# A gated scan followed by a gated convolution unit: four PSUM banks handed out in turn, x loaded apart from its gates, and part of the gated inputs moved to VectorE

## The chip, the core and the metric

The kernel runs on one core of one Trainium2 chip. The profile shows five engines that run side by side, each with its own list of instructions: TensorE (PE) for matmuls and transposes, VectorE (DVE) and ScalarE (ACT) for element-wise work, GpSimd (POOL), and SyncE (SP), which here only issues the transfers. Matmul results land in the memory PSUM, which this kernel lays out as eight banks of 2 KiB per partition; all other tiles are in the memory SBUF. The metric is the device time in microseconds. Some runs fall in a slower state; the ratios below use fast runs alone, against fast runs of the kernel before on the same chip.

## The reference

x, r_gate and i_gate have 4 x 6336 rows of 256 columns (fp32). Cut to what matters:

```
a_t     = exp(8 * sigmoid(r_gate) * log(sigmoid(a_param)))
x_gated = sqrt(max(1 - a_t*a_t, 1e-6)) * sigmoid(i_gate) * x
h_t     = a_t * h_{t-1} + x_gated_t          # scan along the rows, y = all h
gate    = sigmoid(5-tap causal convolution of y, per column)
out     = (gate * (y @ w_val)) @ w_out
```

## The kernel before

Rows come in 51 tiles of 512 rows (three have 256), most of them two to a chunk (28 chunks). The rows lie on the partitions when they are loaded, but the scan wants columns on the partitions, so TensorE transposes three times: the tanh of r (`srT`), the square root (`nT`, back to rows, to multiply it with the gated input) and the product (`xT`, for the scan). Each tile passes these stages; the names are those of the profile:

| Stage | Engine | What it does |
|---|---|---|
| load r, i, x | DMA, queue SP | three transfers of 512 KB a tile |
| tanh | ACT | both gates in one instruction (sigmoid by way of tanh) |
| u2 | POOL | (tanh(i) + 1) * x, two instructions |
| srT, exp | PE, ACT | transpose, then a |
| e | POOL | a * a |
| sq | ACT | square roots, in batches of chunks, as they need another table of functions (each load of a table took 1.28 us) |
| nT, xg | PE, DVE | transpose the root, multiply with u2 |
| xT, scan | PE, DVE | transpose the product, scan into y |
| conv, tg, val, gv | PE, ACT, PE, DVE | convolution, tanh, y @ w_val, product |
| out, osb | PE, DVE or ACT | last matmul, copy from PSUM |
| store | DMA, queue SP | 512 KB a tile |

A planner in the kernel file (a list scheduler with a cost for each job and a priority for each kind) fixes the order of each engine's instructions before anything is built. On the chip an engine waits, but does not overtake. The parts that the change touches (shortened; the comments are not in the kernel):

```python
UNITS = [3, 1, 3, 3, 2, 3, 2, 3, 2, 2, 1, 1, 1, 1]      # chunks in each batch of square roots
NS, NY, NIN, NTRI, NXG, NOSB = 10, 6, 3, 4, 3, 3        # buffers
# ... cut
        ri = inp.tile([P, 2, SUB, D], FP32, name="ri", tag="ri", bufs=NIN)
        xt = inp.tile([P, SUB, D], FP32, name="xt", tag="xt", bufs=NIN)
        nc.sync.dma_start(ri[:, 0, 0:nj, :], ...)        # r, then i, then x: always together
# ... cut
            nc.gpsimd.tensor_scalar(out=t1, in0=tri[:, 1], scalar1=1.0, scalar2=1.0, op0=ALU.mult, op1=ALU.add)
            nc.gpsimd.tensor_tensor(out=uring[:, g % NS], in0=t1, in1=xt, op=ALU.mult)
# ... cut: one PSUM bank for each purpose
            srT = psum.tile([P, CHUNK], BF16, name="srT", tag="srT", bufs=1)
            nT = psum.tile([P, SUB, D], BF16, name="nT", tag="nT", bufs=1)
            xT = psum.tile([P, CHUNK], BF16, name="xT", tag="xT", bufs=1)
            ops = psum.tile([P, 2, D], FP32, name="ops", tag="ops", bufs=1)
```

The other four banks hold the convolution (two) and y @ w_val (two), before and after.

Of the kernel before, what the change touches and what calls it, by code (L numbers as in the profile page):

```python
# [8 lines left out]
P = 128  # L9
WIN = 512  # L10
# [7 lines left out]
UNITS = [3, 1, 3, 3, 2, 3, 2, 3, 2, 2, 1, 1, 1, 1]  # L18
NS = 10
NY = 6  # L20
NIN = 3
NTRI = 4
NXG = 3
NOSB = 3

OSB = ("DDAADDDADDDDDDDDDDADADDDDDDDDADDADDDDDDDADDDDDDDADDDADDADAADADADADDDADDDDDADADADDAAAAAADDA"
       "DDDDAAAAA")

COST = dict(load=(0.1, 3.8), tanh=(0.2, 1.7), u2=(0.25, 3.15), srT=(0.05, 0.45), exp=(0.35, 0.86), e=(0.1, 1.8),
# [3 lines left out]
PRIO = dict(load=5.07, store=4.64, tanh=5.95, exp=3.94, sq=0.63, tg=0.73, srT=3.16, nT=4.77, xT=-1.91,  # L33
            conv=3.92, val=4.01, out=-0.12, e=4.3, u2=4.55, xg=-0.64, scan=3.88, gv=4.0, osb=-0.43)
# [7 lines left out]
class Shape:  # L42
# [3 lines left out]
    def __init__(self, total, seq):  # L46
        self.chunks, self.tiles, self.chunk_of = [], [], []
        self.seq, self.total = seq, total
        t = 0
        for c, parts in enumerate(CHUNKS):  # L50
            self.chunks.append((t, sum(parts), len(self.tiles), len(self.tiles) + len(parts)))
            for n in parts:
                self.tiles.append((t, n))
                self.chunk_of.append(c)
                t += n
        assert t == total
        self.apos, self.aold = self.place(NS * WIN)
        self.ypos, self.yold = self.place(NY * WIN)
        self.pieces = [(g, i) for g, (_, n) in enumerate(self.tiles) for i in range(n // (2 * P))]
# [17 lines left out]
def make_jobs(sh):  # L77


    jobs = {op: [] for op in PRIO}  # L80
# [4 lines left out]
    def job(op, eng, f, deps, cost=None):  # L85
        fix, per = COST[cost or op]
        jobs[op].append((eng, fix + per * f, [d for d in deps if d[1] >= 0]))

    for g, (_, n) in enumerate(sh.tiles):
        f = n / WIN  # L90
        c = sh.chunk_of[g]
        job("load", "DMA", f, [("tanh", g - NIN), ("u2", g - NIN)])
        job("tanh", "ACT", f, [("load", g), ("u2", g - NTRI)]
            + ([("srT", 2 * sh.chunk_of[g - NTRI] + 1)] if g >= NTRI else []))
        job("u2", "POOL", f, [("tanh", g)] + [("xg", g - NS)])
        job("nT", "PE", f, [("sq", unit_of[c]), ("xg", g - 1)])
        job("xg", "DVE", f, [("nT", g), ("u2", g)] + ([("xT", 2 * sh.chunk_of[g - NXG] + 1)] if g >= NXG else []))
        job("conv", "PE", f, [("scan", 2 * c + 1), ("tg", g - 1)])
        job("tg", "ACT", f, [("conv", g), ("gv", g - 2)])
        job("val", "PE", f, [("scan", 2 * c + 1), ("gv", g - 1), ("conv", g)])  # L100
        job("gv", "DVE", f, [("tg", g), ("val", g)] + ([("out", qlast[g - 2])] if g >= 2 else []))
        job("store", "DMA", f, [("osb", qlast[g])])
    for c, (_, n, g0, g1) in enumerate(sh.chunks):
        f = n / CHUNK
        yo = sh.yold[c]
        ylast = sh.chunks[yo][3] if yo >= 0 else -1
        for h in range(2):
            k = 2 * c + h
            job("srT", "PE", f, [("tanh", g1 - 1), ("exp", k - 1)])
            aold = ("scan", 2 * sh.aold[c] + h if sh.aold[c] >= 0 else -1)  # L110
            job("exp", "ACT", f, [("srT", k), aold])
            job("e", "POOL", f, [("exp", k), aold])
            job("xT", "PE", f, [("xg", g1 - 1), ("scan", k - 1)])
            job("scan", "DVE", f, [("xT", k), ("val", ylast - 1), ("conv", ylast)])
    for q, (g, i) in enumerate(sh.pieces):
        job("out", "PE", 1, [("gv", g), ("osb", q - 1)])
        job("osb", "DVE" if OSB[q] == "D" else "ACT", 1, [("out", q), ("store", g - NOSB)], "osb" + OSB[q])
    for u, n in enumerate(UNITS):
        size = sum(sh.chunks[c][1] for c in range(ends[u] - n, ends[u])) / CHUNK
        fix, per = COST["sq"]  # L120
        jobs["sq"].append(("ACT", fix * n + per * size, [("e", 2 * ends[u] - 1)]))
# [3 lines left out]
def make_plan(sh):  # L125


    jobs = make_jobs(sh)
    nxt = dict.fromkeys(jobs, 0)
    done, free, order, mode = {}, {}, [], "E"  # L130
    while True:
        best = None
        for op, todo in jobs.items():
# [3 lines left out]
            eng, dur, deps = todo[i]  # L137
            t = free.get(eng, 0.0)
            for d in deps:
# [5 lines left out]
            else:  # L145
                if best is None or (t, PRIO[op]) < best[:2]:
                    best = (t, PRIO[op], op, i, eng, dur)
        if best is None:
            break
        t, _, op, i, eng, dur = best  # L150
# [5 lines left out]
        done[op, i] = t + dur + (DMA_LAT if eng == "DMA" else 0.0)  # L156
        order.append((t, op, i, eng, dur))
# [3 lines left out]
    return order  # L161
# [3 lines left out]
def kernel(  # L165
# [23 lines left out]
    plan = make_plan(shape)  # L189
# [5 lines left out]
    def load(g):  # L195
# [3 lines left out]
        xt = inp.tile([P, SUB, D], FP32, name="xt", tag="xt", bufs=NIN)  # L199

        nc.sync.dma_start(ri[:, 0, 0:nj, :], rf[t0:t0 + nt, :].rearrange("(p j) d -> p j d", j=nj))
        for dst, src in ((ri[:, 1, 0:nj, :], if_), (xt[:, 0:nj, :], xf)):
            nc.sync.dma_start(dst, src[t0:t0 + nt, :].rearrange("(j p) d -> p j d", p=P))
        live["ri", g], live["xt", g] = ri, xt

    with tc.manual_schedule():
# [4 lines left out]
        for g in range(NIN):  # L211
            load(g)
# [42 lines left out]
        wo2 = const.tile([P, H, D], BF16, name="wo2")  # L255
        nc.vector.tensor_scalar(out=wo2[:], in0=wo[:], scalar1=0.5, scalar2=None, op0=ALU.mult)
# [3 lines left out]
        psum = ctx.enter_context(tc.tile_pool(name="psum", bufs=1, space=bass.MemoryType.PSUM))  # L260

        aring = rings.tile([P, H, NS * WIN], FP32, name="aring")
        ering = rings.tile([P, H, NS * WIN], FP32, name="ering")
        nring = ering[:].bitcast(BF16)
        uring = rings.tile([P, NS, SUB, D], BF16, name="uring")
# [10 lines left out]
        def op_load(g, eng):  # L276
            if g >= NIN:
                load(g)

        def op_tanh(g, eng):  # L280
            nj = tiles[g][1] // P
            ri = live.pop(("ri", g))
            tri = inp.tile([P, 2, SUB, D], BF16, name="tri", tag="tri", bufs=NTRI)
            nc.scalar.activation(out=tri[:, :, 0:nj, :], in_=ri[:, :, 0:nj, :], func=ACT.Tanh, scale=0.5)  # L284
            live["tri", g] = tri

        def op_u2(g, eng):
            nj = tiles[g][1] // P
            xt, tri = live.pop(("xt", g)), live["tri", g]
            t1 = work.tile([P, SUB, D], FP32, name="t1", tag="t1", bufs=1)  # L290
            nc.gpsimd.tensor_scalar(out=t1[:, 0:nj, :], in0=tri[:, 1, 0:nj, :], scalar1=1.0, scalar2=1.0,  # L291
                                    op0=ALU.mult, op1=ALU.add)
            nc.gpsimd.tensor_tensor(out=uring[:, g % NS, 0:nj, :], in0=t1[:, 0:nj, :], in1=xt[:, 0:nj, :],  # L293
                                    op=ALU.mult)

        def op_srT(k, eng):
            c, h = k // 2, k % 2
            srT = psum.tile([P, CHUNK], BF16, name="srT", tag="srT", bufs=1)
            transposes(srT, [(live["tri", g][:, 0], tiles[g][1] // P) for g in range(*chunks[c][2:])], h)
# [10 lines left out]
        def op_e(k, eng):  # L310
            c, h = k // 2, k % 2
            nt, a0 = chunks[c][1], shape.apos[c]
            a = aring[:, h, a0:a0 + nt]
            nc.gpsimd.tensor_tensor(out=ering[:, h, a0:a0 + nt], in0=a, in1=a, op=ALU.mult)  # L314

        def op_sq(u, eng):
            for c in range(sum(UNITS[:u]), sum(UNITS[:u + 1])):
                nt, a0 = chunks[c][1], shape.apos[c]
                nc.scalar.activation(out=nring[:, :, 2 * a0:2 * a0 + nt], in_=ering[:, :, a0:a0 + nt],  # L319
                                     func=ACT.Sqrt, scale=-0.25, bias=b025[:, 0:1])  # L320

        def op_nT(g, eng):
            c = chunk_of[g]
            n0 = 2 * shape.apos[c] + tiles[g][0] - chunks[c][0]
            nT = psum.tile([P, SUB, D], BF16, name="nT", tag="nT", bufs=1)
            for j in range(tiles[g][1] // P):
                for h in range(H):
# [4 lines left out]
        def op_xg(g, eng):  # L332
            nj = tiles[g][1] // P
            xg = work.tile([P, SUB, D], BF16, name="xg", tag="xg", bufs=NXG)
            nc.vector.tensor_tensor(out=xg[:, 0:nj, :], in0=live.pop(("nT", g))[:, 0:nj, :],  # L335
                                    in1=uring[:, g % NS, 0:nj, :], op=ALU.mult)
            live["xg", g] = xg

        def op_xT(k, eng):
            c, h = k // 2, k % 2  # L340
            xT = psum.tile([P, CHUNK], BF16, name="xT", tag="xT", bufs=1)
            transposes(xT, [(live["xg", g], tiles[g][1] // P) for g in range(*chunks[c][2:])], h)
# [73 lines left out]
        def op_out(q, eng):  # L416
            g, i = pieces[q]
            gv = live["gv", g]
            ops = psum.tile([P, 2, D], FP32, name="ops", tag="ops", bufs=1)
            for e in range(2):  # L420
                for hk in range(H):
                    nc.tensor.matmul(out=ops[:, e, :], lhsT=gv[:, 2 * i + e, hk, :], rhs=wo2[:, hk, :],  # L422
# [3 lines left out]
        def op_osb(q, eng):  # L426
            g, i = pieces[q]
            if i == 0:
                live["osb", g] = work.tile([P, SUB, D], FP32, name="osb", tag="osb", bufs=NOSB)
            dst = live["osb", g][:, 2 * i:2 * i + 2, :]  # L430
# [12 lines left out]
        ops_by_name = dict(load=op_load, tanh=op_tanh, u2=op_u2, srT=op_srT, exp=op_exp, e=op_e, sq=op_sq,  # L443
# [34 lines left out]
```

## Time and profile before

| | Before |
|---|---|
| Device time, median | 340.5 us (339.4 to 342.5, 4 runs) |
| Span of the profiled run | 338.6 us |
| Busy: ACT, POOL, PE, DVE | 302.8, 266.5, 252.6, 247.2 us |
| Moved | 104.56 MB, 309 GB/s over the span |
| Last load issued (x of the last tile) | 285.5 us |

Busy time counts all instructions of an engine, waits left out. The prediction below shows and reads the lines of the slices, of three stretches of time, and of the waits. Here is only one stretch more: from 40 to 260 us. The columns are the same as there (stretch, its length, busy time of PE, PE weight load, DVE, ACT, POOL, granted clock, DMA share, GB/s):

```profile
40.00:260.00 220.00, 177.30 (x2100) 118.63 (x2098) 173.69 (x162) 205.59 (x159) 198.54 (x114) 0.91 0.98 340
```

ACT and POOL are at 93% and 90%, DVE at 79%, and 340 GB/s move.

### The profile page before, as it was taken

What the parts mean: (1) busy time and instruction counts of PE and PEld (TensorE: products, weight loads), DVE (VectorE), ACT (ScalarE), POOL (GpSimd) and SP (SyncE); (2) the same over time, 40 slices, a digit from 0 to 9 for tenths busy, and PEclk for the clock granted to TensorE, in tenths of its full rate; (3) what the DMA queues carried; (4) which work ended last, traced back from release to release, by engine and by line L of the source; (5) the groups of instructions that cost most, each with busy time, mean ns of one, the idle gap of its engine ahead of it and who ended that gap; (6) DMA issues with size and microseconds to landing.
All of it is one profiled execution on the core that took longest, in us unless ns stands there. A gap on an engine that the chain in (4) does not pass through costs nothing.

```text
span 338.6 us, 7417 instructions
## 1 busy us (share of the span) xinstructions
PE 252.6 (75%) x2987; PEld 166.9 (49%) x2987; DVE 247.2 (73%) x251; ACT 302.8 (89%) x251; POOL 266.5 (79%) x170
## 2 busy tenths in 40 slices
PE   1122578962599699969973996995998997989894
PEld 0111444531466456646642664663665664565553
DVE  3000487840559959999973799995999998999992
ACT  6558998988979989999989899999999999999883
POOL 6699799999799867989996997998797799551100
PEclk9999997995559969999997799999999999999998
DMA  7999969999998979999999999999999999332334
GB/s 174 340 366 367 360 228 349 346 369 398 333 295 271 298 262 315 332 381 381 391 381 400 353 298 313 375 351 373 343 340 389 382 324 361 127 133 117 126 126 187
DMA packets 68432, 104.56 MB, mean 309 GB/s; under 512 B 4391, under 2 KB 55342, under 8 KB 68398
## 3 DMA queue, kind: packets, MB, share of 16 engines
q1 hardware_dynamic: 67022, 103.83, 87.6%
q0 software_dynamic: 1376, 0.26, 0.9%
q8 instruction: 23, 0.38, 0.5%
q14 instruction: 11, 0.09, 0.1%
HBM read 78.39 MB, written 25.95 MB: 308 GB/s over the span
## 4 chain that ended last, share of the span: by engine, by line
PE 28%; ACT 23%; DVE 18%; DMA 17%; issue 12%; SPq 2%; ACTq 0%; DVEq 0%
DMA ri<-in_i_gate_dram 14%; PE gp L384 10%; DVE yring L358 8%; ACT tri L284 6%; PE ops L422 5%; PE val L400 4%; ACT tg L392 4%; DVE gv L410 4%; ACT ering L319 4%; DVE osb L433 4%; PE xT L272 4%; ACT aring L306 3%; PE srT L272 3%; PE nT L328 2%; ACT L392 2%
## 5 line engine op out<-in xcount | busy, mean ns | idle before, releaser
L314 POOL TENSOR_TENSOR ering<-aring 128x1024 f32<-128x1024 f32 (+2 forms) x56 | 94.4, 1695 | 40.8 <-ACT aring L306 36.0
L293 POOL TENSOR_TENSOR uring<-t,xt 128x1024 bf16<-128x1024 f32 (+1 forms) x51 | 117.1, 2296 | 4.3
L358 DVE TENSOR_TENSOR_SCAN yring<-aring,yring,xT 128x1024 bf16<-128x1024 f32 (+5 forms) x54 | 111.1, 2057 | 11.5 <-PE xT L272 10.8
L284 ACT ACTIVATE tri<-ri 128x2048 bf16<-128x2048 f32 (+1 forms) x51 | 94.7, 1865 | 9.8 <-DMA ri<-in_i_gate_dram 9.3
L384 PE MATMUL gp<-yring,diag 64*64 64x512 bf16 (+16 forms) x1196 | 71.4, 363 | 9.3 <-ACT tg L392 7.9
L306 ACT ACTIVATE aring<-srT,khf 128x1024 f32<-128x1024 bf16 (+2 forms) x56 | 62.5, 1116 | 8.6 <-PE srT L272 5.6
L422 PE MATMUL ops<-wo,gv 128*128 128x256 bf16 x396 | 60.8, 277 | 10.2 <-DVE osb L433 6.2
L410 DVE SCALAR_TENSOR_TENSOR gv<-tg,val 128x1024 bf16<-128x1024 bf16 (+1 forms) x54 | 60.5, 1126 | 9.5 <-ACT tg L392 5.8
L335 DVE TENSOR_TENSOR xg<-nT,uring 128x1024 bf16<-128x1024 bf16 (+1 forms) x51 | 33.8, 662 | 40.9 <-PE nT L328 26.4
L272 PE MATMUL srT<-ident_b,tri 128*128 128x128 bf16 x396 | 35.9, 236 | 35.4 <-ACT tri L284 20.5
L291 POOL TENSOR_SCALAR t<-tri 128x1024 f32<-128x1024 bf16 (+1 forms) x51 | 52.0, 1020 | 10.4 <-ACT tri L284 4.5
L392 ACT ACTIVATE tg<-gp 128x1024 bf16<-128x1024 f32 (+1 forms) x51 | 51.3, 1006 | 5.0 <-PE gp L384 4.8
L433 DVE COPY osb<-ops 128x512 f32<-128x512 f32 x67 | 45.6, 680 | 13.9 <-PE ops L422 13.8
L400 PE MATMUL val<-yring,wv 128*128 128x512 bf16 (+1 forms) x204 | 51.8, 377 | 3.6 <-DVE gv L410 3.5
L319 ACT ACTIVATE ering<-ering,b 128x2048 bf16<-128x2048 f32 (+2 forms) x28 | 50.5, 1804 | 1.0
L384 PEld LDWEIGHTS <-diag 64*64 64x64 bf16 x1196 | 33.4, 111 | 34.2 <-issue 20.1
L272 PEld LDWEIGHTS <-tri 128*128 128x128 bf16 x396 | 27.9, 105 | 44.5 <-ACT tri L284 23.7
L422 PEld LDWEIGHTS <-gv 128*128 128x128 bf16 x396 | 36.1, 99 | 26.1 <-issue 15.6
L328 PE MATMUL nT<-ident_b,ering 128*128 128x128 bf16 x396 | 34.3, 235 | 12.8 <-ACT ering L319 7.6
L272 PE MATMUL xT<-ident_b,xg 128*128 128x128 bf16 x396 | 34.7, 231 | 8.7 <-DVE yring L358 6.3
L272 PEld LDWEIGHTS <-xg 128*128 128x128 bf16 x396 | 27.0, 103 | 22.0 <-issue 14.8
L328 PEld LDWEIGHTS <-ering 128*128 128x128 bf16 x396 | 27.8, 106 | 19.3 <-ACT ering L319 8.9
(31 smaller groups left out, 95.0 us busy)
## 6 DMA issues: line engine op xcount, KB each, us to landing
ri<-in_r_gate_dram SPq DMA_DIRECT2D x48, 512.0 KB, 6.7
ri<-in_i_gate_dram SPq DMA_DIRECT2D x48, 512.0 KB, 7.8
xt<-in_x_dram SPq DMA_DIRECT2D x48, 512.0 KB, 7.0
out_dram<-osb SPq DMA_DIRECT2D x48, 512.0 KB, 6.0
ri<-in_r_gate_dram SPq DMA_DIRECT2D x3, 256.0 KB, 4.6
ri<-in_i_gate_dram SPq DMA_DIRECT2D x3, 256.0 KB, 6.0
xt<-in_x_dram SPq DMA_DIRECT2D x3, 256.0 KB, 4.8
out_dram<-osb SPq DMA_DIRECT2D x3, 256.0 KB, 2.0
```

What stands on the lines that cost most here:

```text
L272: nc.tensor.transpose(out=dst[:, col:col + P], in_=src[:, j, h * P:(h + 1) * P], identity=ident_b[:])
L284: nc.scalar.activation(out=tri[:, :, 0:nj, :], in_=ri[:, :, 0:nj, :], func=ACT.Tanh, scale=0.5)
L293: nc.gpsimd.tensor_tensor(out=uring[:, g % NS, 0:nj, :], in0=t1[:, 0:nj, :], in1=xt[:, 0:nj, :], op=ALU.mult)
L306: nc.scalar.activation(out=aring[:, h, a0:a0 + nt].rearrange("c (w p j) -> c w p j", p=P, j=nj), in_=live.pop(("srT", k))[:, 0:nt].rearran ...
L314: nc.gpsimd.tensor_tensor(out=ering[:, h, a0:a0 + nt], in0=a, in1=a, op=ALU.mult)
L328: nc.tensor.transpose(out=nT[:, j, h * P:(h + 1) * P], in_=nring[:, h, n0 + j * P:n0 + (j + 1) * P], identity=ident_b[:])
L358: nc.vector.tensor_tensor_scan(out=yring[:, h, y0 + c0:y0 + c1], data0=aring[:, h, a0 + c0:a0 + c1], data1=xT[:, c0:c1], initial=0.0 if fr ...
L384: nc.tensor.matmul(out=gp[64 * h:64 * h + 64, m, c0:c1], lhsT=diag[rows, h, kk, rows], rhs=yring[rows, h, src:src + c1 - c0], start=(sh == 0),
L392: nc.scalar.activation(out=tg[:, :, 0:nt], in_=live.pop(("gp", g))[:, :, 0:nt], func=ACT.Tanh, scale=0.5)
L400: nc.tensor.matmul(out=val[:, m, 0:nt], lhsT=wv[:, hk, m * P:(m + 1) * P], rhs=yring[:, hk, y0:y0 + nt], start=(hk == 0), stop=(hk == H - 1))
L410: nc.vector.scalar_tensor_tensor(out=gv[:, 0:nj, hs, :].rearrange("c j h p -> c j (h p)"), in0=tg[:, hs, 0:nt].rearrange("c h (p j) -> c j ...
L422: nc.tensor.matmul(out=ops[:, e, :], lhsT=gv[:, 2 * i + e, hk, :], rhs=wo2[:, hk, :], start=(hk == 0), stop=(hk == H - 1))
```

## The change

Its intent: transposes and outputs should wait less for a bank, loads of the gates should not wait for buffers of x, GpSimd should be relieved, and work on VectorE should begin earlier. The diff, cut to its core (comments added; `NIN` is not changed):

```diff
-UNITS = [3, 1, 3, 3, 2, 3, 2, 3, 2, 2, 1, 1, 1, 1]
+UNITS = [2, 2, 1, 3, 3, 3, 3, 3, 2, 2, 1, 3]
-NTRI = 4
-NXG = 3
 NIN = 3                       # now for the gates alone
+NX = 5                        # x, with its own loads
+NTR = 3                       # tanh of r
+NTI = 6                       # tanh of i
+BANKS = 4
+PB = dict(srT=2, nT=2, xT=2, ops=2)     # so many of one kind at a time
+U2 = "PDPDDDDPPPPDDDPPDPPDPPPPPPPPPPPPPPPPDPPPPPPPPPDPPPP"
 ... cut: OSB and PRIO get other values
+            if need:                     # planner: a job that writes PSUM takes the bank free first
+                b = min(bank_free)
 ... cut
-            srT = psum.tile([P, CHUNK], BF16, name="srT", tag="srT", bufs=1)
+            srT = bank(banks["srT", k], BF16)          # likewise nT, xT and the output
 ... cut
+            if eng == "DVE":
+                nc.vector.scalar_tensor_tensor(out=u, in0=ti, scalar=1.0, in1=xt, op0=ALU.add, op1=ALU.mult)
+                return
 ... cut: square roots of neighbouring chunks become one instruction; xg is written in place
```

## The prediction

> **What bounds the kernel now.** I first read the busy times, then the slices of the span, to see whether one engine is the limit throughout.
>
> ```profile
> PE 252.6 (75%) x2987; PEld 166.9 (49%) x2987; DVE 247.2 (73%) x251; ACT 302.8 (89%) x251; POOL 266.5 (79%) x170
> ...
> DVE  3000487840559959999973799995999998999992
> ACT  6558998988979989999989899999999999999883
> POOL 6699799999799867989996997998797799551100
> ...
> GB/s 174 340 366 367 360 228 349 346 369 398 333 295 271 298 262 315 332 381 381 391 381 400 353 298 313 375 351 373 343 340 389 382 324 361 127 133 117 126 126 187
> ```
>
> No engine is full throughout. ACT (ScalarE) is nearest with 89%. DVE (VectorE) does almost nothing in the first four of the 40 slices and is full only from about slice 22 on. POOL (GpSimd) is the reverse: full in the loading part, idle at the end. The last row shows that the loads are over after 34 slices (about 288 us); then only stores run, at 110 to 190 GB/s. Asked for the three stages that this suggests, the trace answers:
>
> ```profile
> 0.00:34.30 34.30, 6.59 (x43) 4.22 (x43) 3.33 (x18) 22.56 (x20) 27.71 (x29) 1.00 1.01 312
> 34.30:290.00 255.70, 205.66 (x2452) 137.53 (x2452) 203.66 (x193) 240.99 (x187) 225.39 (x130) 0.92 0.98 342
> 290.00:338.60 48.60, 40.32 (x496) 25.19 (x492) 40.22 (x42) 39.24 (x46) 13.41 (x13) 0.98 0.33 131
> ```
>
> Columns: stretch and its length; busy us of PE, PE weight load, DVE, ACT and POOL; granted clock, DMA share, GB/s. In the head DVE works 3.3 of 34.3 us. In the middle ACT works 94% of the time, POOL 88%, DVE and PE 80%. In the tail of 48.6 us PE, DVE and ACT share the work left over, 81 to 83% each. So the end is set by work that came late: DVE began its main work at 34.3 us and afterwards lost more time waiting. Next, who waited for whom (total us, times, longest):
>
> ```profile
> DVE xg L335 <- PE nT L328: 26.4, 9, 20.9
> DVE osb L433 <- PE ops L422: 13.8, 15, 2.5
> DVE yring L358 <- PE xT L272: 11.3, 12, 3.0
> DVE xg L335 <- POOL uring L293: 9.7, 1, 9.7
> ```
> ```profile
> ACT tri L284 <- DMA ri<-in_i_gate_dram: 9.3, 7, 2.4
> ACT aring L306 <- PE srT L272: 5.6, 10, 0.9
> ACT osb L435 <- PE ops L422: 5.4, 6, 1.5
> ```
> ```profile
> SPq L203 <- POOL uring L293: 77.4, 38, 5.0
> SPq L440 <- DVE osb L433: 76.3, 31, 5.4
> ```
>
> The 20.9 us is the head itself. The other rows of DVE's list are smaller; all waits after the head add up to 54 us, which agrees with busy time (299.3 us from 34.3 to its last instruction at 333.6, less 243.9 busy = 55). About 31 of the 54 are DVE waiting for PE to fill the single bank of xT, ops or nT (11.3 + 13.8 + 26.4 - 20.9); 14 are POOL (9.7, and 3.9 and 0.8 in rows not shown). PE's own list has the other half of the ping-pong: srT waits 14.9 us for the exponential that empties its bank, ops 6.2 and 3.6 for the output copies, xT 6.3 for the scan, nT 5.1 for xg. The last two rows are the load queue, which works in order: it stands 77 us at the issue of x because GpSimd has not released a buffer, and 76 us at stores, with loads queued behind them.
>
> **What the Trainium skill says.** "PSUM — Partial Sum Buffer", summary of rules for kernel authors: if PSUM is to be read while a matmul runs, aim the matmul at a different bank. The trace agrees as to the cost of one bank per purpose: the waits in both directions just listed. "GPSIMD Engine Reference", section 4.1: elementwise work belongs on VectorE, GpSimd being about twice as slow with two inputs. The trace agrees with a wider gap: adding one and multiplying takes GpSimd 1045 + 2360 ns for a 128x1024 tile, while DVE's comparable fused instruction (gv) takes 1215 ns. The same page's section 8, key points, says that GpSimd shares SBUF interfaces with VectorE and contends with DVE instructions having two SBUF inputs. No run here shows it: xg, gv and the scan each take one tensor from PSUM. The moved instruction would be the first main DVE instruction with two tensors in SBUF. "ScalarE activation tables: per-element evaluation and per-set limits", section "What a function is on this engine", has one table load between sets at 1283 ns; the trace agrees, its 31 loads last 1283 ns each. The rows that I size the parts with (busy us, mean ns of one, idle before):
>
> ```profile
> L410 DVE SCALAR_TENSOR_TENSOR gv<-tg,val 128x1024 bf16<-128x1024 bf16 x48 | 58.3, 1215 | 8.0 <-ACT tg L392 5.8 <-PE ops L422 1.5 <-PE val L400 0.7
> ...
> L319 ACT ACTIVATE ering<-ering,b 128x2048 bf16<-128x2048 f32 x23 | 46.1, 2002 | 1.0
> ...
> L319 ACT ACTIVATE ering<-ering,b 128x1024 bf16<-128x1024 f32 x2 | 2.3, 1148 | 0.0
> ```
>
> **The change part by part.** Counts are from the instruction lists of both builds.
>
> GpSimd loses 12 of its 51 gated inputs: 12 x (1.045 + 2.360) = 41 us, 266.5 to about 226. It stops being a limit of the loading stage. All but two of the twelve are among tiles 1 to 19, where DVE had idle time.
>
> DVE gains these 12 at gv's 1.215 us: +14.6. Output copies on DVE go from 67 to 69: +1.4. Main work becomes 243.9 + 16.0 = 259.9 us.
>
> ACT has 25 table loads in place of 31, as the square roots come in fewer batches: 6 x 1.283 = -7.7. The square roots become 15 instructions instead of 28, because neighbours in the ring are joined. From 1148 and 2002 ns at 1024 and 2048 elements a fixed part of 0.29 us follows: 13 x 0.29 = -3.8. Two output copies fewer at 0.59: -1.2. ACT becomes 302.8 - 12.7 = 290.1 us.
>
> PE does the same 2987 matmuls, and the same 104 MB move.
>
> The head. The first square root now needs two chunks (768 rows) instead of three (1792), and follows the third tanh. Before, the third tanh ended at 18.6 us; 0.75 MB less (x of tiles 0 and 1) now lies ahead of its input, 2 us at 350 GB/s. So the square root may start at about 18, after a table load, take 1.6, and then come the transposes (0.6). But x of tile 0 is issued behind the fifth pair of gate loads, hence after the second tanh; with landing and GpSimd's turn that is about 21. I take 22 us for the first xg instead of 34.3: 12 us earlier.
>
> DVE's waits. The four banks are no more than before, only handed to whoever comes next, so I let half of the 31 us of bank ping-pong go (-15), and all of the 14 us for GpSimd. 54 - 29 = 25 remain. A shared bank brings a new wait: PE is in order, and a transpose whose turn brings a bank that a late reader still holds stops all behind it. I allow +8, as an estimate.
>
> The sum on DVE's path: 22 (start) + 260 (work) + 25 + 8 (waits) + 5 (last gv to the last store landed, 338.6 - 333.6 before) = 320 us of span. On ACT's: idle before is 338.6 - 302.8 = 35.8; of it the waits for gates (9.3, which the earlier gate loads should cut to about 3) and for banks (5.6 + 5.4, halved) give back 12: 290 + 24 = 314. The two are coupled, and the later one counts. Of the span the device time is 2 us more (340.4 against 338.6 in the profiled run), while a few of my waits overlap. I say 319.
>
> **The rivals.** First: the DMA engines become the bound, and the other gains are hidden. For it: their share is 0.98 in the middle, and about 97.7 MB (all inputs, three quarters of the output) must pass before the tail. Against: the stretch runs at 342 GB/s on average, while single slices reach 381 to 400; the share counts time of packets in flight, not capacity. At 388 GB/s, 97.7 MB take 252 us, 36 less than now. If transfers held 350 GB/s instead, loads would end at 281, and with a tail of 46 the span would be 327 us. Separate x also puts more stores and x loads in one ordered queue, so this rival could cost more.
>
> Second: DVE takes over from GpSimd as limit. It would have 260 us of work in some 290 us; in its best stretch before, 200 to 320 us, it worked 93% of the time. If it fell to its 80% of the middle stage, the work would take 325 us, and the span would be longer than before: 22 + 325 + 5 = 352. Against: those 80% contain just the waits on banks and GpSimd that the change attacks. If only half of the expected cut in waits comes, the time is about 333.
>
> Third: contention of the moved instructions with GpSimd. At worst GpSimd stands still while they run, 14.6 us, and it has some 41 us to spare: worth 0 to 3 us.
>
> Fourth: everything goes well, ACT alone limits and it idles for only 18 us: 290 + 18 = 308.
>
> **Range and chances.** 308 is the good rival and 333 the half-effective one; I put 80% on 308 to 332. Faster by over 2% means under 334.4, which holds unless both the DMA and the DVE rival come true: 0.91. Within 2%: 0.07. Slower: 0.02.
>
> **What would show it.** In the changed profile GpSimd should be busy for about 226 us, ACT 290 with 25 table loads, DVE 263; the moved instruction should last about 1.2 us. The first xg should start at 20 to 25 us. Waits of DVE for xT, ops and nT after the head should total some 15 us instead of 31, those for GpSimd near zero, and the load queue should hardly wait for GpSimd's tile any more. GB/s should be over 360 through the loading stage, and loads should end at about 272 us. The prediction is wrong if loads end later than 285 with the rate unchanged (then DMA or its order binds), if DVE's waits come back under another name, such as PE waiting for a bank, or if DVE still starts after 30.

## The result, and the profile after

The changed kernel takes 323.89 us (median of 4 runs, 323.18 to 325.87) against 340.51: a ratio of 0.9515, 95% interval 0.945 to 0.958. Ratios here are the mean time of one kernel's fast runs over that of the other's of the same rounds, so not quite the ratio of the medians quoted. The prediction was 319, range 308 to 332.

The page of the profile after, the lines that answer to those in the prediction:

```profile
PE 246.5 (76%) x2987; PEld 161.6 (50%) x2987; DVE 270.2 (83%) x265; ACT 289.5 (89%) x230; POOL 236.1 (73%) x146
...
DVE  3126649999899699999999679988987997999993
...
POOL 6427552999899759996599999999995790299200
...
GB/s 217 349 363 375 330 338 357 363 316 389 342 368 385 381 306 342 355 389 400 381 337 404 392 381 310 401 387 395 374 389 377 344 280 169 131 101 161 131 197 194
```

VectorE is at work from the third slice on and nearly full from the seventh. Before, it reached 9 tenths first in slice 13, fell to 3 to 7 tenths again in slices 21 to 23, and stayed near full only from slice 24 on, with one dip. The rate of transfers falls from slice 33 on, before from slice 35 on; a slice is 8.1 us now, 8.5 before. Three stages again, here cut where VectorE starts and where the last load is issued (before, the second cut lay 4.5 us after that issue), and then the stretch of 40 to 260 us:

```profile
0.00:21.54 21.54, 3.71 (x27) 2.78 (x27) 4.33 (x18) 17.30 (x16) 10.09 (x18) 1.00 0.99 303
21.54:277.00 255.46, 201.35 (x2449) 133.59 (x2450) 224.68 (x207) 235.91 (x172) 206.47 (x112) 0.96 1.00 355
277.00:324.10 47.10, 41.41 (x515) 25.27 (x512) 41.21 (x42) 36.25 (x44) 19.52 (x16) 0.99 0.40 158
```

```profile
40.00:260.00 220.00, 174.26 (x2172) 115.92 (x2176) 198.41 (x181) 203.55 (x148) 186.99 (x102) 0.97 1.03 367
```

In 40 to 260 us the transfers run at 367 instead of 340 GB/s, and VectorE works 198 instead of 174 us, while ScalarE and TensorE do about what they did and GpSimd somewhat less. All four are now at 79 to 93%. Who VectorE and the load queue wait for:

```profile
DVE uring L394 <- PE bank L387: 9.6, 10, 4.3
...
DVE osb L490 <- PE bank L479: 7.4, 10, 2.2
DVE uring L350 <- DMA xt<-in_x_dram: 6.2, 4, 2.6
DVE uring L394 <- POOL uring L354: 6.1, 1, 6.1
...
DVE yring L415 <- PE bank L327: 0.9, 3, 0.6
```

```profile
SPq L497 <- DVE osb L490: 91.6, 38, 5.7
SPq L248 <- ACT tring L343: 48.6, 27, 4.1
...
SPq L255 <- POOL uring L354: 21.0, 11, 4.5
```

VectorE's waits for transposes and output fall from 31 to 9.6 + 7.4 + 0.9 = 17.9 us. Its one wait for GpSimd (6.1) lies before the first xg. A new one appears: 6.2 us for x, by the moved instructions themselves. The load queue waits 21 us for GpSimd at the issue of x instead of 77, but 92 instead of 76 for output copies on VectorE and 49 instead of 17 for the tanh that empties a buffer of the gates (second line): the queue still works in order, and much of its waiting has moved to other engines. Then the groups that were to cost 1.2 us each:

```profile
L374 POOL TENSOR_TENSOR ering<-aring 128x1024 f32<-128x1024 f32 x46 | 89.9, 1978 | 38.2 <-ACT aring L366 30.2 <-ACT ering L378 7.9
...
L467 DVE SCALAR_TENSOR_TENSOR gv<-tg,val 128x1024 bf16<-128x1024 bf16 x48 | 58.0, 1209 | 5.9 <-PE val L457 3.6 <-ACT tg L449 2.2
...
L350 DVE SCALAR_TENSOR_TENSOR uring<-tring,xt 128x1024 bf16<-128x1024 bf16 x12 | 23.1, 1939 | 6.2 <-DMA xt<-in_x_dram 6.2
```

The moved instruction (last line) takes 1939 ns on average, the same operation with one tensor in PSUM (gv) 1209. GpSimd's square takes 1978 ns where it took 1894 before.

Where the 14.5 us of span went (between the two profiled runs; by the medians of device time it is 16.6) can be read at the last load. These are the lines of the load queue's timeline in which the last load is issued, first of the kernel before, then of the changed one (start us, us, engine, line):

```profile
285.54 0.38 SPq L203 DMA_DIRECT2D xt<-in_x_dram  x1
```

```profile
277.40 0.78 SPq L249 DMA_DIRECT2D ri<-in_i_gate_dram  x1
```

The last load is issued 8.1 us earlier, and the tail after that issue is 324.1 - 277.4 = 46.7 us instead of 338.6 - 285.5 = 53.1, so 6.4 less. The two make the 14.5.

### The profile page after: what moved, and what is told of

It reads as the page before. It is cut to its first block, busy times and chain, and to the rows that moved or that the text cites. A ratio compares the mean times of both kernels' runs of the same rounds, so it can differ in the third digit from the quotient of the medians.

```text
span 324.1 us, 7354 instructions
## 1 busy us (share of the span) xinstructions
PE 246.5 (76%) x2987; PEld 161.6 (50%) x2987; DVE 270.2 (83%) x265; ACT 289.5 (89%) x230; POOL 236.1 (73%) x146
## 4 chain that ended last, share of the span: by engine, by line
ACT 20%; DVE 18%; PE 18%; DMA 17%; issue 14%; POOL 10%; SPq 2%; ACTq 0%; DVEq 0%; POOLq 0%
DMA ri<-in_i_gate_dram 10%; DVE yring L415 9%; DMA xt<-in_x_dram 7%; ACT tring L343 6%; PE bank L479 5%; ACT ering L378 4%; POOL ering L374 4%; PE gp L441 4%; POOL uring L354 4%; PE val L457 3%; ACT tg L449 3%; PE bank L327 3%; DVE gv L467 3%; DVE osb L490 3%; DVE uring L394 3%
## 5 line engine op out<-in xcount | busy, mean ns | idle before, releaser
L374 POOL TENSOR_TENSOR ering<-aring 128x1024 f32<-128x1024 f32 (+2 forms) x56 | 97.5, 1765 | 44.6 <-ACT aring L366 36.5
L415 DVE TENSOR_TENSOR_SCAN yring<-aring,yring,bank 128x1024 bf16<-128x1024 f32 (+5 forms) x54 | 109.4, 2046 | 0.4 <-PE bank L327 0.4
L343 ACT ACTIVATE tring<-ri 128x2048 bf16<-128x2048 f32 (+1 forms) x51 | 93.9, 1865 | 10.0 <-DMA ri<-in_i_gate_dram 9.6
L479 PE MATMUL bank<-wo,gv 128*128 128x256 bf16 x396 | 58.1, 279 | 10.5 <-DVE gv L467 3.7
L366 ACT ACTIVATE aring<-bank,khf 128x1024 f32<-128x1024 bf16 (+2 forms) x56 | 59.4, 1109 | 6.2 <-PE bank L327 5.6
L490 DVE COPY osb<-bank 128x512 f32<-128x512 f32 x69 | 45.6, 679 | 8.6 <-PE bank L479 7.4
L479 PEld LDWEIGHTS <-gv 128*128 128x128 bf16 x396 | 36.7, 99 | 29.4 <-issue 14.6
L378 ACT ACTIVATE ering<-ering,b 128x2048 bf16<-128x2048 f32 (+3 forms) x15 | 46.7, 3112 | 2.3 <-POOL ering L374 1.9
L441 PEld LDWEIGHTS <-diag 64*64 64x64 bf16 x1196 | 31.6, 108 | 32.6 <-issue 17.4
L353 POOL TENSOR_SCALAR t<-tring 128x1024 f32<-128x1024 bf16 (+1 forms) x39 | 45.0, 1154 | 2.0
L394 DVE TENSOR_TENSOR uring<-bank,uring 128x1024 bf16<-128x1024 bf16 (+1 forms) x51 | 33.0, 666 | 15.9 <-PE bank L387 9.6
L327 PE MATMUL bank<-ident_b,tring 128*128 128x128 bf16 x396 | 32.1, 232 | 17.3 <-ACT tring L343 12.5
L327 PEld LDWEIGHTS <-tring 128*128 128x128 bf16 x396 | 26.0, 104 | 25.9 <-ACT tring L343 14.2
L327 PE MATMUL bank<-ident_b,uring 128*128 128x128 bf16 x396 | 31.9, 224 | 8.9 <-DVE uring L394 6.0
```

Of the source, the lines that this page charges most:

```text
L327: nc.tensor.transpose(out=dst[:, col:col + P], in_=src[:, j, h * P:(h + 1) * P], identity=ident_b[:])
L343: nc.scalar.activation(out=tring[:, r:i + 1:i - r, 0:nj, :], in_=ri[:, :, 0:nj, :], func=ACT.Tanh, scale=0.5)
L366: nc.scalar.activation(out=aring[:, h, a0:a0 + nt].rearrange("c (w p j) -> c w p j", p=P, j=nj), in_=live.pop(("srT", k))[:, 0:nt].rearran ...
L374: nc.gpsimd.tensor_tensor(out=ering[:, h, e0:e0 + nt], in0=a, in1=a, op=ALU.mult)
L378: nc.scalar.activation(out=nring[:, :, 2 * e0:2 * e0 + m], in_=ering[:, :, e0:e0 + m], func=ACT.Sqrt, scale=-0.25, bias=b025[:, 0:1])
L415: nc.vector.tensor_tensor_scan(out=yring[:, h, y0 + c0:y0 + c1], data0=aring[:, h, a0 + c0:a0 + c1], data1=xT[:, c0:c1], initial=0.0 if fr ...
```

## The experiments

Twelve kernels ran, each unprofiled run in three rounds against the kernel before on the same chip (one had a single look). "Same order" means that each engine's order of work is frozen as the planner made it for the changed kernel; "order made anew" means that the planner ran again under the altered rule. "Searched" means that priorities, batches and shares of work were searched for that rule with the planner's own cost table. In a search the cost of a gated input on VectorE was set to 1.9 us.

| Kernel | Median us | Ratio to before, 95% interval |
|---|---|---|
| changed kernel | 323.9 | 0.9515 (0.945 to 0.958) |
| u2_pool_same_order | 335.9 | 0.9893 (0.982 to 0.997) |
| retuned_all_gpsimd | 335.0 | 0.9892 (0.984 to 0.994) |
| own_banks_replanned | 357.1 | 1.0511 (1.041 to 1.061) |
| retuned_own | 332.5 | 0.9798 (0.975 to 0.984) |
| retuned_shared | 328.9 | 0.9653 (0.957 to 0.974) |
| late_first_sqrt | 323.6 | 0.9543 (0.945 to 0.963) |
| half_xg (wrong) | 323.4 | 0.9553 (0.949 to 0.961) |
| half_exp (wrong) | 323.5 | 0.9518 (0.945 to 0.959) |
| two_taps (wrong) | 321.8 | 0.9480 (0.941 to 0.956) |
| no_add (wrong) | 321.2 | 0.9436 (0.939 to 0.948) |
| half_x_bytes (wrong) | 319.2 | 0.9437 (0.938 to 0.950) |

### The moved inputs, back on GpSimd

```diff
-            ops_by_name[op](i, eng)
+            ops_by_name[op](i, "POOL" if op == "u2" else eng)
```

> The 12 gated inputs go back from VectorE to GpSimd, each at its place in the same order of all other work. Theory A (VectorE's path sets the end, and the 12 moved instructions cost it 23 us because each takes 1.9 us): VectorE's busy time falls from 270 to about 247, GpSimd's rises from 236 to about 267, and the time stays within 322 to 328 us, because what VectorE gains it spends waiting for GpSimd. Theory B (moving them off GpSimd was what freed the loading stage): the time goes back to 332 or more, with VectorE's waits for GpSimd over 10 us. Theory C (the move was a loss): under 320 us.

Measured: 335.9 us. GpSimd's busy time is 266.5 us, as in the kernel before, VectorE's falls to 248.8, and the last gate load is issued at 287.9 us instead of 277.4. VectorE waits for GpSimd again:

```profile
DVE uring L394 <- POOL uring L354: 19.9, 4, 6.8
```

The profile also follows a chain back from the last instruction, at each step to what released it. Its shares of the span, first in this run, then in the kernel before:

```profile
POOL 44%; issue 15%; DMA 14%; PE 11%; ACT 10%; DVE 4%; SPq 1%; POOLq 0%; DVEq 0%; ACTq 0%
```

```profile
PE 28%; ACT 23%; DVE 18%; DMA 17%; issue 12%; SPq 2%; ACTq 0%; DVEq 0%
```

Theory B holds for this order, and GpSimd leads its chain. In the kernel before GpSimd is not in the chain at all, although it held up the load queue for 77 us; that it set the pace there is argued, not shown. All the rest of the change together, without this move, is worth 1.1% (ratio 0.9893).

An order searched for this split could have been better:

> Shared banks, all 51 gated inputs on GpSimd, with an order searched for that. Theory A (GpSimd at 266 us of work paces the loading stage, whatever the order): 332 us or more. Theory B (only the unadapted order made u2_pool_same_order slow; VectorE is relieved by 23 us): 320 to 326 us.

It was not: 335.0 us, GpSimd again at 266.5, ScalarE waiting 18.7 us for gates. With 266 us on GpSimd two quite different orders end within 1 us of each other, though in this one GpSimd has only 10% of the chain.

### One bank for each purpose

```diff
-PB = dict(srT=2, nT=2, xT=2, ops=2)
+PB = dict(srT=1, nT=1, xT=1, ops=1)
+OWN = dict(srT=0, nT=1, xT=2, out=3)
-                b = min(bank_free)
+                b = bank_free[OWN[op]]
-            banks[op, i] = bank_free.index(min(bank_free))
+            banks[op, i] = OWN[op]
```

The frozen order cannot be tried with own banks: played through from the plan it deadlocks, so there is no run of it (nT of tile 12 stands right behind nT of tile 11 and would wait for a reader that, on VectorE, stands behind work that needs a later matmul). So the order was made anew.

> Each purpose (srT, nT, xT, output) gets its one PSUM bank back; all else as in the changed kernel, the order made anew under that rule. Theory A (half of the bank waits went because banks are shared): VectorE's waits for PE's transposes and output rise from 18 to about 30 us, and the time is 332 to 338 us. Theory B (the waits went because of the earlier start and the other order): the time stays within 322 to 328 us.

Measured: 357.1 us, slower than the kernel before and outside both theories' numbers. VectorE's waits for xT, output and nT are 13.0, 14.2 and 9.5 us, 36.7 together, near the 30 of theory A; in addition its gv waits 6.9 us for the last matmul. But the priorities had been searched for shared banks, so this run tells of the two together. Hence a search for own banks:

> One PSUM bank for each purpose again, but now with an order searched for that rule (priorities, batches, the shares of VectorE and ScalarE), as the changed kernel's order was searched for shared banks. Theory A (sharing the four banks is itself worth several per cent): 332 us or more. Theory B (the 357 us of own_banks_replanned came from an order made for another rule): 322 to 330 us.

Measured: 332.5 us, at the edge of theory A (ratio 0.9798). Most of the excess of the 357 was the unadapted order. How much of the remaining 8.6 us belongs to the banks depends on how good a search is, and that was tested by searching for the whole change again:

> The change in whole, with an order searched anew after the cost of a gated input on VectorE was set to 1.9 us instead of 1.2 (14 of them there, spread over more of the run; 11 batches of square roots). If the order of the changed kernel lost time because it was made with too low a cost: 315 to 321 us. If the order makes no more difference: 322 to 327 us.

Measured: 328.9 us, 5 us worse than the order that the change came with, although the planner's own figure had become better (320.4 us against 325.9 with the corrected cost, both got by running the planner of the kernel files). It gave retuned_all_gpsimd 315.9, the best figure of the three, and that took 335.0. So the planner ranks orders only to some 3%. The fair comparison for the banks is between two orders of the same kind of search, by the ratios, as the runs were on different chips: 0.9798 against 0.9653, 1.5%. The two intervals (0.957 to 0.974 and 0.975 to 0.984) just miss each other. But the changed kernel and retuned_shared, two orders under one rule for the banks and nearly the same split (12 and 14 gated inputs on VectorE), differ by 1.4% themselves, so 1.5% between two single orders does not show that the banks are the cause. The move off GpSimd, compared in the same way, is worth 0.9892 - 0.9653 = 2.4%. No version here with a right result is clearly faster than the changed kernel.

### A late start of VectorE

```diff
-UNITS = [2, 2, 1, 3, 3, 3, 3, 3, 2, 2, 1, 3]
+UNITS = [3, 1, 1, 3, 3, 3, 3, 3, 2, 2, 1, 3]
```

> The first batch of square roots takes three chunks as in the kernel before (1792 rows instead of 768), the second and third one each; all else as in the changed kernel. Theory A (VectorE's start stands at the head of the path that sets the end): VectorE's first xg moves from 21.5 to some 30 us and the time rises by 5 to 9 us, to 329 to 333. Theory B (there is slack later that absorbs a late start): 323 to 326 us.

Measured: 323.6 us. The first xg of the changed kernel and of this one in VectorE's timeline:

```profile
21.54 0.42 DVE L394 TENSOR_TENSOR uring<-bank,uring 128x512 bf16<-128x512 bf16 x1 [6.11 <-POOL uring L354]
```

```profile
36.82 0.42 DVE L394 TENSOR_TENSOR uring<-bank,uring 128x512 bf16<-128x512 bf16 x1 [20.34 <-PE bank L387]
```

VectorE starts 15.3 us later, later even than in the kernel before, and the end does not move. In 40 to 80 us it works 38.2 of 40 us where it worked 35.0 in the changed kernel, and the last load is issued at 278.4 us, within 1 us of 277.4. The batches are an input of the planner, so the order was made anew here: compared from the two kernel files, it differs in the first two fifths of VectorE's jobs and not after. With an order that fits it, then, a late start costs nothing; in the frozen order it was not tried. The early start fills VectorE's first slices, but the work that it brings forward was not what the end waited for.

### The disputed instruction alone

This kernel computes nothing useful. Line 256 is the moved operation alone, 260 GpSimd's square alone; 267 and 269 are these two side by side; 276 is the moved operation beside GpSimd's add of one; 285 has its second tensor in PSUM, beside the square.

> No useful result, wrong on purpose: five phases that measure one instruction each. Theory A (a VectorE instruction with two tensors in SBUF shares a read port with GpSimd): alone 1.2 us per 128x1024 tile; beside GpSimd's square 1.8 to 2.8, and GpSimd's own instruction longer than its 1.9 alone; with one tensor in PSUM beside GpSimd's square again 1.2. Theory B (the long ones in the kernel come from DMA traffic or from the strided tile): 1.2 in all phases.

The groups of instructions (busy us, mean ns, idle before):

```profile
L267 DVE SCALAR_TENSOR_TENSOR u<-ti,xt 128x1024 bf16<-128x1024 bf16 x12 | 27.4, 2287 | 0.4
L276 DVE SCALAR_TENSOR_TENSOR u<-ti,xt 128x1024 bf16<-128x1024 bf16 x12 | 22.7, 1893 | 0.4
L278 POOL TENSOR_SCALAR t<-ti 128x1024 f32<-128x1024 bf16 x12 | 21.8, 1820 | 0.9
L269 POOL TENSOR_TENSOR e<-ga 128x1024 f32<-128x1024 f32 x8 | 21.2, 2645 | 0.6
L287 POOL TENSOR_TENSOR e<-ga 128x1024 f32<-128x1024 f32 x8 | 15.1, 1892 | 0.5
L260 POOL TENSOR_TENSOR e<-ga 128x1024 f32<-128x1024 f32 x8 | 15.1, 1892 | 0.5
L285 DVE SCALAR_TENSOR_TENSOR u<-ti,pb 128x1024 bf16<-128x1024 bf16 x12 | 14.6, 1220 | 0.4
L256 DVE SCALAR_TENSOR_TENSOR u<-ti,xt 128x1024 bf16<-128x1024 bf16 x8 | 9.8, 1224 | 0.2
L262 POOL TENSOR_SCALAR t<-ti 128x1024 f32<-128x1024 bf16 x8 | 8.4, 1044 | 0.6
```

The two instructions side by side once more, as shortest/median/longest in ns:

```profile
L267 DVE SCALAR_TENSOR_TENSOR u<-ti,xt x12: 1216/2797/2966, 42.0 to 68.5; 128x1024 bf16<-128x1024 bf16 x12
```

```profile
L269 POOL TENSOR_TENSOR e<-ga x8: 1887/2752/2754, 43.2 to 62.2; 128x1024 f32<-128x1024 f32 x8
```

Alone the moved operation takes 1224 ns, as predicted from gv. Beside the square its mean is 2287, but three of the twelve ran after the last square; the median is 2797, and that of the square 2752 instead of 1892. One after the other the two would take 3.1 us, side by side they take 2.8: they hardly overlap. Beside the add of one (278) the moved operation takes 1893, and the add 1820 instead of 1044 (262), both as means. With one tensor in PSUM it takes 1220, and the square is not slowed (287). What theory A forecast holds: both sides pay when VectorE reads two tensors from SBUF while GpSimd works. That a read port is what they share was not tested apart.

### Relief of one engine at a time

The five kernels below keep the order of the changed kernel and take work away from one engine, or bytes from the loads. If one of these alone sets the pace, the time must fall by much of what is taken away.

VectorE:

```diff
-            nc.vector.tensor_tensor(out=u, in0=nT[:, 0:nj, :], in1=u, op=ALU.mult)
+            nc.vector.tensor_tensor(out=u[:, :, 0:P], in0=nT[:, 0:nj, 0:P], in1=u[:, :, 0:P], op=ALU.mult)
```

> The changed kernel in its own order, but VectorE's product xg covers half of the columns (result wrong on purpose): about 15 us less of VectorE's 270. Theory A (VectorE's path, start plus work plus waits, sets the end): 309 to 315 us. Theory B (VectorE only follows what the loads and ScalarE bring, except in the tail): 320 to 324 us.

Measured: 323.4 us. VectorE was busy 259.8 us, 10.4 less (the product itself 20.3 instead of 33.0). What it saved it waited:

```profile
DVE uring L394 <- PE bank L387: 15.0, 13, 6.7
DVE osb L490 <- PE bank L479: 10.5, 11, 2.1
```

ScalarE:

```diff
-   .rearrange("c (w p j) -> c w p j", p=P, j=nj), in_=...
+   .rearrange("c (w p j) -> c w p j", p=P, j=nj)[:, :, 0:ph, :], in_=...   # ph = P // 2 for 21 of the 28 chunks
```

> The changed kernel in its own order, but the exponential of 21 of the 28 chunks covers half of the rows (result wrong on purpose): 16 us less of ScalarE's 289.5. Theory A (ScalarE sets the pace of the loading stage and most of the end): 306 to 314 us. Theory B (no one engine does; what ScalarE saves it spends waiting, as VectorE did in half_xg): 320 to 324 us.

Measured: 323.5 us with ScalarE at 275.0 us, 14.5 less. Its waits for gates rise from 9.6 to 13.0 us and those for the convolution from 6.4 to 10.2.

TensorE:

```diff
-            for kk in range(CONV_K - 1, -1, -1):
+            for kk in (CONV_K - 1, 0):
```

> The changed kernel in its own order, but the convolution uses two of its five taps (result wrong on purpose): some 41 us less of TensorE's 246. Theory A (TensorE, working in order, sets the pace, whatever its busy share of 76% says): 300 to 314 us. Theory B (it does not): 319 to 324 us.

Measured: 321.8 us with TensorE at 218.0 us, 28.5 less (I had expected 41). The interval (0.941 to 0.956) covers the changed kernel's 0.9515.

The loads:

```diff
-        nc.sync.dma_start(xt[:, 0:nt // P, :], xf[t0:t0 + nt, :]...)
+        nc.sync.dma_start(xt[:, 0:nh, :], xf[t0:t0 + nh * P, :]...)      # nh = nt // P // 2
 ... cut: x gets five fixed buffers, zeroed on VectorE at the start
```

> The changed kernel in its own order, but each load of x brings only the first half of its rows (buffers zeroed once at the start; result wrong on purpose): 13.0 MB less of 104.6, same number of loads, all engines' work the same. Theory A (the loading stage runs at the rate of the DMA engines): the loads end some 20 us earlier or more, and the time falls to 305 to 314 us, where ScalarE's 290 us of work take over. Theory B (the engines' chain sets the pace, and loads only follow the buffers that they free): 320 to 325 us.

Measured: 319.2 us, between the two theories. 91.6 MB move instead of 104.6; ScalarE waits 3.7 us for gates instead of 9.6, and the last gate load is issued at 270.9 us, 6.5 earlier. By the medians this is the largest effect of the five kernels of this group, but 12% fewer bytes are worth 1.4% (0.8% by the ratios, whose intervals overlap with the changed kernel's, so it is not clear of the noise). The zeroing costs VectorE some 5 us more work, 275.0 instead of 270.2.

GpSimd, the last one open:

```diff
-            t1 = ...
-            nc.gpsimd.tensor_scalar(out=t1, in0=ti, scalar1=1.0, scalar2=1.0, op0=ALU.mult, op1=ALU.add)
-            nc.gpsimd.tensor_tensor(out=u, in0=t1, in1=xt, op=ALU.mult)
+            nc.gpsimd.tensor_tensor(out=u, in0=ti, in1=xt, op=ALU.mult)
```

> The changed kernel in its own order, but GpSimd leaves out the add of one before its product (result wrong on purpose): 39 instructions, 45 us less of GpSimd's 236. Theory A (GpSimd still paces the loading stage: its buffers of x set when loads start): VectorE's moved instructions get shorter too, and the time falls to 305 to 315 us. Theory B (after the change no engine paces the kernel alone, as half_xg, half_exp and two_taps showed for the three others): 318 to 323 us, a part of it from less contention at the shared port.

Measured: 321.2 us with GpSimd at 183.4 us, 53 less. Its waits for x rise from 9 to 36 us and those for the exponential from 36.5 to 61. The moved instructions on VectorE get only a little shorter, 1803 ns instead of 1939. Theory B holds. With the runs above this gives three points for one engine in one frozen order: GpSimd busy 266 us, time 335.9; 236 us, 323.9; 183 us, 321.2. The first 30 us of relief buy 12 us, the next 53 buy 2.7 (0.8% by the ratios, not clear of the noise).

## Why the prediction was right or wrong

**The size and the direction** held: 323.9 us against 319, inside the range, faster by over 2%.

**GpSimd's relief** was rightly named as a cause, and the experiments make it the clearest one: taking the move back costs 12 us (0.9893 against 0.9515) in the frozen order, which was made for the move, and 2.4% between two searched orders, against the 1.4% by which two orders of one rule differ. The size of its term was off. The step was "12 x (1.045 + 2.360) = 41 us, 266.5 to about 226"; the measured busy time is 236.1, because GpSimd's own instructions became longer.

**VectorE's added work** was mis-sized for the same reason. "DVE gains these 12 at gv's 1.215 us: +14.6" took a duration from an instruction with one tensor in PSUM. The measured one is 1.939 us on average, 12 x 0.73 = 8.7 us more; port_measure shows such contention with GpSimd, in both directions. The third rival had put this at 0 to 3 us on the time, and had looked only at GpSimd's side.

**The banks.** Waits for transposes and output fell from 31 to 18 us, expected were some 15. That sharing the banks is what gained time is not shown: two searched orders with and without it differ by 1.5%, hardly more than two orders of one rule, and the large loss in own_banks_replanned comes mostly from the order. With shared banks but without the move the kernel gained only 1.1%.

**ScalarE** came out as worked out: 289.5 us against 290.1, with 25 table loads.

**The head** is the step that failed. The time of the first xg was right (21.5 us against 22), but the sum counted "12 us earlier" in full. late_first_sqrt starts VectorE at 36.8 us, in an order made for that, and ends at the same time (323.6 us). The prediction also misread the row of VectorE before, "full only from about slice 22 on": slices 13 to 20 were nearly full but for one, and slices 21 to 23 were the low ones.

**The sum on VectorE's path** failed with it as an explanation, though its number was near, in part by luck. Start, work, waits and end always add up to about the span, on any engine, so that they add up proves nothing: 21.5 + 265.9 + 31.6 + 4.3 = 323.3 us measured, of a span of 324.1, where 265.9 is 270.2 less the 4.3 before the first xg, 31.6 the waits after it, and 4.3 the time from the end of gv to the end of the span. The waits came close to the expected 25 + 8, but 6.2 us of them are for x, which was not foreseen. In the sum the waits were treated as given. half_xg shows that they are not: less work on VectorE is answered by more waiting. The same happened on ScalarE, TensorE and GpSimd. The prediction's "the later one counts" supposed one path that binds; in the changed kernel, with its order frozen, none of the engines does alone. Its lesser error was to write 319 after a sum that gave 320 of span and 2 more of device time.

**The DMA rival** was rightly set aside as the sole bound: 13 MB less moved the end by 4.7 us and not by the 35 us that the bytes take at 367 GB/s. In the loading stage the rate did rise, to 367 GB/s from 40 to 260 us, and to 355 in the middle stage, where "over 360 through the loading stage" had been expected. Loads ended later than the expected 272: the last issue is at 277.4.

**What stays open.** Why the kernel before took 340 us is only known by what taking parts of the change back did; no engine was relieved in that kernel itself. The granted clock of TensorE is a rival that the prediction did not weigh: its mean is 0.936 in the profiled run before and 0.967 after. It does not look like the main part: retuned_all_gpsimd ran at 0.948 to 0.962 and still took 334 to 337 us, and the fastest run of the kernel before took 336.7 us at 0.953. Loading x apart from the gates was not taken back alone, so its share is unknown. Nor was any pair of engines relieved together, which would show how far apart the next limits are. The last gate load is issued right after the queue has stood 10 us at three stores (266.5 to 276.9 us); whether the tail would shrink if it went ahead of them was not run.

## What to carry to other kernels

When a kernel has four engines above 70% and fixed orders, do not add up one engine's start, work and waits and call it the path: take work from one engine (a wrong result will do) and see whether the end moves. Relief of the engine that paces pays at first, and stops paying when the next limit is met, here after about 12 us. When element-wise work is moved from GpSimd to VectorE, look at where its inputs lie: with two tensors in SBUF, both engines slowed down here while they ran side by side (1224 ns to 2797, and GpSimd's 1892 to 2752). And an order that was searched for one rule says little when it is reused under another, nor do two single orders settle a difference of 1 or 2%.

## What the Trainium skill lacked or had wrong

- "GPSIMD Engine Reference", section 8, names the contention for a VectorE instruction with two SBUF inputs but gives no size for it there (the skill's page on SBUF goes further into it). Here: VectorE 1224 ns alone, a median of 2797 beside a two-input GpSimd instruction (itself 1892, then 2752), a mean of 1893 beside a one-input one (1044, then 1820), and 1220 with one tensor in PSUM.
- "ScalarE: Activation LUTs", section "What ACT_TABLE_LOAD costs", puts a switch of tables at 1283 ns plus a drain of about 1380. The trace of the kernel before agrees with the 1283 and shows no such gap around the load: its 14 loads ahead of square roots were preceded by 0.2 us of idle time in all, and the square roots after them by 1.0 us, also in all.
